# Gated linear attention and a cosine-gated MLP on one core: y evicted in token order, and output tiles stored in one transfer each

## The chip, the core and the metric

The kernel runs on one NeuronCore of a Trainium2 chip. Its engines work from queues of their own and meet at semaphores: TensorE (PE, matmuls, with PEld for the loading of weights), VectorE (DVE), ScalarE (ACT), GpSimd (POOL) and SyncE (SP), which here only issues DMA transfers. ACT and POOL can issue transfers too. The metric is the device time of a run in microseconds (us); lower is better. Differences of a few tenths of a per cent matter here.

## The reference

There are 4 batches, 8 heads, 768 tokens and a head dimension of 48. The first half is a recurrence over tokens with a state of 48 x 48 for each head; the second is an MLP over 3072 tokens of 384 features, with 2048 hidden features and a gate h * cos(h).

```
for t in range(S):
    state = alpha[:, :, t, :, None] * state + einsum('bhd,bhe->bhde', k[:, :, t], v[:, :, t])
    y[:, :, t] = einsum('bhd,bhde->bhe', q[:, :, t], state)
x = y.transpose(0, 2, 1, 3).reshape(B * S, H * D)     # tokens x 384
h = x @ w_in
out = (h * cos(h)) @ w_out                            # tokens x 384, float32
```

## The kernel before

The tokens are worked on in 12 pairs J (NJ = 12) of 256 tokens (T2), each of two chunks c of 128 tokens (C); three pairs make a batch. An input transfer (`load`, L105) puts two neighbouring tokens, an even one and an odd one (index e), into one partition. Within a chunk the tokens therefore stand in the order "64 even ones, then 64 odd ones" in everything that follows: masks, scores, y, the hidden features, and the rows of the output tile.

For each pair the attention steps are: logarithms and cumulated sums of alpha, scaling of q and k (`scale_k` L212, `scale_q` L216, on POOL or DVE), a cast of v (`cast_v`, L219, POOL) and a rearrangement of it by four SBUF transfers (`stack_v`, L225, issued by SP), transposes (`trans`, L260) and their evictions (L266), scores (L274) with a mask (L279), the state's update (`outer` L291, `add_state` L305, `decay_state` L313), and `yT` (L340), which leaves y transposed in PSUM: three groups of 128 features on the partitions, tokens along the row. `evict_y` (L350) copies one chunk of it to the bf16 tile xT, once on ACT or DVE for each chunk.

The MLP for a pair: `mlp1` (L359) multiplies w_in with xT in four parts u, ACT takes the sine with a shift of pi/2 (`cosine`, L365), DVE multiplies (`gate`, L370), and `mlp2` (L387) multiplies with w_out, chunk by chunk in four parts, with the gated tile gsb as the stationary operand, so that tokens come out on the partitions. `evict_o` (L396) copies a chunk's 128 x 384 result to SBUF, and `store` (L403) sends it to memory. As partitions 0 to 63 hold even tokens and 64 to 127 odd ones, it issues two transfers for each chunk, of 64 rows that lie two rows apart in memory.

The last chunk of all, (11, 1), is different. `mlp2` (L381) computes its left and right 192 columns apart, in the two banks of one PSUM tile o_last. In each of its four parts there are four matmuls for the left half, then four for the right. `evict_o` (L394) copies the left half on ACT and the right on DVE, into one SBUF tile, and `store` issues four transfers: the even tokens of each half on SP's queue and the odd ones on ACT's.

PSUM has a tag "h" with three tiles of two banks (`two_banks`, used for y, U, the scores, h and o_last), a tag "x" of one bank (the cumulated sums of a pair) and a tag "o" of one bank (the outputs). Each o_sb tile is one of four buffers.

The order of the work is written out by hand: a table PLAN gives every step of every pair a number, the steps are issued sorted by it, and each engine executes its own in that order. SP's queue thus holds loads, rearrangements of v and stores in one sequence: a store that waits for its eviction, or whose issue takes long, holds back the loads behind it.

Of the kernel before, what the change touches and what calls it, by code (L numbers as in the profile page):

```python
# [9 lines left out]
FP = mybir.dt.float32  # L10
# [6 lines left out]
def kernel(  # L17
# [10 lines left out]
    nc = tc.nc  # L28
    B, H, S, D = q.shape
    DM, DF = moe_w_in.shape  # L30
    C = 128
    HC = C // 2
    T2 = 2 * C
    NJB = S // T2
    NJ = B * NJB
    NP = H // 2
    HD = H * D
    KT = DM // C
# [9 lines left out]
    sb = ctx.enter_context(tc.tile_pool(name="sb", bufs=2))  # L48
    ps = ctx.enter_context(tc.tile_pool(name="ps", bufs=1, space=bass.MemoryType.PSUM))
# [14 lines left out]
    for c in range(2):  # L64
        r = slice(HC * c, HC * c + HC)
# [14 lines left out]
    for lst, nm, n in ((lna_t, "lna", NL), (kh_t, "kh", NQ), (qh_t, "qh", NQ), (vp_t, "vp", NV)):  # L80
        for r in range(n):
            t = consts.tile([C, 2, H, 64], BF, tag=f"{nm}{r}", name=f"{nm}{r}")
            nc.vector.memset(t[:, :, :, D:64], 0.0)
            lst.append(t)
    for r in range(NS):
        t = consts.tile([C, 2, H, 64], BF, tag=f"vs{r}", name=f"vs{r}")
# [8 lines left out]
    w2 = consts.tile([C, NF, DM], BF, tag="w2", name="w2")  # L95

    a_sb, kqv, cp_sb, icp_sb, qkT_sb, A_sb, c2_sb = {}, {}, {}, {}, {}, {}, {}
    xT, gsb = {}, {}
# [72 lines left out]
    def two_banks(name):  # L171
        return ps.tile([C, 2, 512], FP, tag="h", name=name, bufs=3)
# [78 lines left out]
    T_ps, A_ps, y_ps, U_ps = {}, {}, {}, {}  # L251
# [95 lines left out]
    def evict_y(J, c, copy):  # L347
        if J not in xT:
            xT[J] = sb.tile([C, KT, T2], BF, tag="xT", name="xT", bufs=BUF["xT"])
        copy(out=xT[J][:, :, c * C : (c + 1) * C], in_=y_ps[J][:, c, 0 : KT * C].rearrange("r (i t) -> r i t", i=KT))  # L350

    h_ps, c_sb, o_ps, o_sb = {}, {}, {}, {}

# [19 lines left out]
    HALVES = [slice(0, DM // 2), slice(DM // 2, DM)]  # L373

    def mlp2(J, c, part):
        if (J, c) == (NJ - 1, 1):
            if part == 0:
                o_ps[J, c] = two_banks("o_last")
            for z, cols in enumerate(HALVES):
                for ft in range(part * NF // MP, (part + 1) * NF // MP):  # L380
                    nc.tensor.matmul(o_ps[J, c][:, z, 0 : DM // 2], gsb[J][:, ft, c * C : (c + 1) * C], w2[:, ft, cols],  # L381
                                     start=(ft == 0), stop=(ft == NF - 1))
            return
        if part == 0:
            o_ps[J, c] = ps.tile([C, 512], FP, tag="o", name="o_ps", bufs=1)
        for ft in range(part * NF // MP, (part + 1) * NF // MP):
            nc.tensor.matmul(o_ps[J, c][:, 0:DM], gsb[J][:, ft, c * C : (c + 1) * C], w2[:, ft],  # L387
                             start=(ft == 0), stop=(ft == NF - 1))

    def evict_o(J, c, copy):  # L390
        o_sb[J, c] = sb.tile([C, DM], FP, tag="o_sb", name="o_sb", bufs=4)
        if (J, c) == (NJ - 1, 1):
            for z, cp in enumerate((nc.scalar.copy, nc.vector.tensor_copy)):
                cp(out=o_sb[J, c][:, HALVES[z]], in_=o_ps[J, c][:, z, 0 : DM // 2])  # L394
        else:
            copy(out=o_sb[J, c], in_=o_ps.pop((J, c))[:, 0:DM])  # L396

    def store(J, c):
        rows = out[J * T2 + c * C : J * T2 + (c + 1) * C, :].rearrange("(i e) d -> e i d", e=2)
        for cols in HALVES if (J, c) == (NJ - 1, 1) else [slice(0, DM)]:  # L400
            for e in range(2):
                eng = nc.scalar if (J, c, e) == (NJ - 1, 1, 1) else nc.sync
                eng.dma_start(out=rows[e][:, cols], in_=o_sb[J, c][HC * e : HC * e + HC, cols])  # L403

    idle_ps = []

    def idle(n):
# [12 lines left out]
        "vev": lambda J, eng="DVE": evict_vs(J, copies[eng]), "decay": decay, "trans": trans,  # L420
        "evT": lambda J, c, eng="DVE": evict_T(J, c, copies[eng]), "scores": scores, "mask": mask, "outer": outer,
        "add": add_state, "state": decay_state, "yT": yT, "evy": lambda J, c, eng="ACT": evict_y(J, c, copies[eng]),
        "m1": mlp1, "sin": cosine, "gate": gate, "m2": mlp2, "evo": lambda J, c, eng="ACT": evict_o(J, c, copies[eng]),
        "out": store, "idle": idle,
    }

# [70 lines left out]
    for key, line in PLAN.items():  # L497
        kind, *rest = key.split()
        for J, word in enumerate(line.split()):
            if word != "-":  # L500
                t, _, eng = word.partition(":")
# [38 lines left out]
```

## Time and profile before

| | us |
|---|---|
| median of 3 runs | 189.28 (189.15 to 189.62) |
| the profiled execution | 189.54 |
| its span, from first to last instruction | 187.5 |
| PE busy in the span | 176.4 |
| DVE, ACT, POOL busy | 134.8, 125.3, 77.8 |

The span is what the page and the trace show; about 2 us of the execution lie outside it. A row of "groups of instructions" gives line, engine, operation, output and inputs, shapes and count, then the busy time in us and the mean of one in ns, then the idle time of the engine just before and what ended it. In the order of time the columns are start, duration, engine, line, operation and count. For a stretch, each engine's busy time comes with the count in brackets, then the granted clock of PE, the busy share of the DMA engines (it can pass 1) and GB/s. SPq and ACTq are the queues in which SP and ACT issue transfers; the time of such a row is that of the issue, not of the transfer, whose time from issue to landing is given apart.

### The profile page before, as it was taken

What the parts mean: (1) busy time and instruction counts of PE and PEld (TensorE: products, weight loads), DVE (VectorE), ACT (ScalarE), POOL (GpSimd) and SP (SyncE); (2) the same over time, 40 slices, a digit from 0 to 9 for tenths busy, and PEclk for the clock granted to TensorE, in tenths of its full rate; (3) what the DMA queues carried; (4) which work ended last, traced back from release to release, by engine and by line L of the source; (5) the groups of instructions that cost most, each with busy time, mean ns of one, the idle gap of its engine ahead of it and who ended that gap; (6) DMA issues with size and microseconds to landing.
All of it is one profiled execution on the core that took longest, in us unless ns stands there. A gap on an engine that the chain in (4) does not pass through costs nothing.

```text
span 187.5 us, 5788 instructions
## 1 busy us (share of the span) xinstructions
PE 176.4 (94%) x2469; PEld 126.2 (67%) x2469; DVE 134.8 (72%) x184; ACT 125.3 (67%) x161; POOL 77.8 (42%) x110
## 2 busy tenths in 40 slices
PE   7888799998999999999999999999999999999990
PEld 2434678664577776775598668586776787776880
DVE  7178785589799899588748986885876766573550
ACT  2456876799598977779668999728956182372510
POOL 5079510267564733693895168830540310100000
PEclk9999999999999999999999999999999999999997
DMA  6999999999979958997699944600052004411303
GB/s 146 261 259 166 181 204 237 256 270 258 244 197 290 258 137 206 266 255 185 156 275 257 264 108 101 168 0 3 3 118 69 0 23 108 113 31 45 84 0 84
DMA packets 60537, 29.47 MB, mean 157 GB/s; under 512 B 51424, under 2 KB 60512, under 8 KB 60512
## 3 DMA queue, kind: packets, MB, share of 16 engines
q1 hardware_dynamic: 56640, 25.86, 59.8%
q0 software_dynamic: 3712, 3.15, 11.0%
q8 instruction: 19, 0.31, 0.7%
q10 hardware_dynamic: 160, 0.10, 0.2%
q14 instruction: 6, 0.05, 0.1%
HBM read 25.17 MB, written 4.72 MB: 159 GB/s over the span
## 4 chain that ended last, share of the span: by engine, by line
PE 57%; ACT 16%; DVE 7%; DMA 6%; POOL 5%; SPq 4%; issue 3%; POOLq 0%; DVEq 0%
PE h_ps L359 25%; PE o_ps L387 20%; ACT c_sb L365 4%; PE y_ps L340 3%; DMA a<-in_alpha_dram 3%; DMA v<-in_v_dram 3%; ACT qkT L266 3%; DVE gsb L370 3%; ACT L136 2%; SPq L225 2%; PE T_ps L260 2%; ACT L365 2%; PE A_ps L274 2%; ACT icp L192 2%; ACT cp L200 2%
## 5 line engine op out<-in xcount | busy, mean ns | idle before, releaser
L370 DVE TENSOR_TENSOR gsb<-h_ps,c_sb 128x1024 bf16<-128x1024 f32 x48 | 58.1, 1221 | 21.8 <-ACT c_sb L365 21.0
L365 ACT ACTIVATE c_sb<-h_ps,halfpi 128x1024 bf16<-128x1024 f32 x48 | 53.1, 1114 | 26.8 <-PE h_ps L359 22.9
L359 PE MATMUL h_ps<-xT,w 128*128 128x256 bf16 x576 | 66.7, 273 | 0.9 <-ACT xT L350 0.5
L387 PE MATMUL o_ps<-w,gsb 128*128 128x384 bf16 x368 | 66.7, 327 | 0.0
L359 PEld LDWEIGHTS <-w 128*128 128x128 bf16 x576 | 55.6, 98 | 9.9 <-issue 1.4
L387 PEld LDWEIGHTS <-gsb 128*128 128x128 bf16 x368 | 33.8, 98 | 21.2 <-DVE gsb L370 0.6
L313 POOL TENSOR_TENSOR un<-us,c 128x384 bf16<-128x384 f32 x20 | 16.7, 837 | 40.1 <-DVE us L305 33.8
L279 DVE TENSOR_TENSOR A_sb<-A_ps,msk 128x1024 bf16<-128x1024 f32 x24 | 28.9, 1217 | 1.7 <-PE A_ps L274 1.7
L212 POOL TENSOR_TENSOR kh<-k,icp 128x384 bf16<-128x384 f32 x17 | 16.9, 1000 | 8.8 <-ACT icp L192 8.8
L216 POOL TENSOR_TENSOR qh<-q,cp 128x384 bf16<-128x384 f32 x15 | 15.4, 1031 | 10.5 <-ACT cp L200 10.5
L149 POOL TENSOR_TENSOR a<-a 128x384 f32<-128x384 f32 x9 | 9.3, 1038 | 12.8 <-DMA a<-in_alpha_dram 12.8
L219 POOL CAST vp<-v 128x768 bf16<-128x768 f32 x12 | 10.1, 842 | 10.0 <-DMA v<-in_v_dram 9.9
L141 ACT ACTIVATE lna<-a 128x768 bf16<-128x768 f32 x12 | 10.2, 847 | 4.7 <-DMA a<-in_alpha_dram 4.7
L266 ACT COPY qkT<-T_ps 128x1024 bf16<-128x1024 bf16 x8 | 8.0, 1016 | 7.1 <-PE T_ps L260 4.9
L411 PE MATMUL idle_ps<-zeros 128*128 128x512 bf16 x40 | 11.5, 431 | 1.2 <-DVE zeros L52 1.2
L136 ACT ACT_TABLE_LOAD x9 | 11.5, 1283 | 0.9 <-PEq L524 0.7
L266 DVE COPY qkT<-T_ps 128x1024 bf16<-128x1024 bf16 x16 | 10.8, 683 | 1.7 <-ACT qkT L266 1.7
L365 ACT ACT_TABLE_LOAD x9 | 11.5, 1283 | 0.2
L305 DVE TENSOR_TENSOR us<-U_ps,un 128x384 f32<-128x384 f32 x16 | 8.7, 550 | 3.8 <-PE U_ps L291 2.8
L396 DVE COPY o_sb<-o_ps 128x384 f32<-128x384 f32 x12 | 6.6, 552 | 6.6 <-PE o_ps L387 6.6
L274 PE MATMUL A_ps<-qkT 48*128 48x128 bf16 x192 | 9.2, 218 | 1.0 <-ACT vs L239 0.6
L396 ACT COPY o_sb<-o_ps 128x384 f32<-128x384 f32 x11 | 5.3, 479 | 7.0 <-PE o_ps L387 5.2
(69 smaller groups left out, 155.5 us busy)
## 6 DMA issues: line engine op xcount, KB each, us to landing
k<-in_k_dram SPq DMA_DIRECT2D x12, 384.0 KB, 5.4
a<-in_alpha_dram SPq DMA_DIRECT2D x12, 384.0 KB, 5.9
v<-in_v_dram SPq DMA_DIRECT2D x12, 384.0 KB, 5.8
q<-in_q_dram SPq DMA_DIRECT2D x12, 384.0 KB, 5.9
out_dram<-o_sb SPq DMA_DIRECT2D x46, 96.0 KB, 3.1
vs<-vp SPq DMA_DIRECT2D x36, 64.0 KB, 2.3
w<-in_moe_w_out_dram POOLq DMA_DIRECT2D x4, 384.0 KB, 10.0
w<-in_moe_w_in_dram POOLq DMA_DIRECT2D x4, 384.0 KB, 7.2
```

The source lines that it names most:

```text
L136: nc.scalar.preload_act_table_set("natural_log_exp_and_others")
L212: eng.tensor_tensor(out=kh_t[J % NQ][:, e, :, 0:D], in0=kqv["k", J][:, :, e], in1=icp_, op=ALU.mult)
L216: eng.tensor_tensor(out=qh_t[J % NQ][:, e, :, 0:D], in0=kqv["q", J][:, :, e], in1=cp, op=ALU.mult)
L266: copy(out=qkT_sb[J][:, c], in_=T_ps[J][:, c].rearrange("r n e s -> r n (e s)"))
L274: nc.tensor.matmul(A_ps[J, c][:, a, p, :], qkT[r, c, NP + p, :], qkT[r, c, p, :], start=True, stop=True)
L279: nc.vector.tensor_tensor(out=A_sb[J][:, c].rearrange("s a p t -> s (a p) t"), in0=A_ps.pop((J, c)).rearrange("s a p t -> s (a p) t"), in1 ...
L313: nc.gpsimd.tensor_tensor(out=u, in0=U_sum.pop(n), in1=c2_sb[J][:, :, c].unsqueeze(3).to_broadcast([C, NP, 2, D]), op=ALU.mult)
L359: nc.tensor.matmul(h_ps[J, u][:, f, :], w1[:, kk, ft * C : (ft + 1) * C], xT[J][:, kk, :], start=(kk == 0), stop=(kk == KT - 1))
L365: nc.scalar.activation(out=c_sb[J, u], in_=h_ps[J, u], func=AF.Sin, bias=halfpi, scale=1.0)
L370: nc.vector.tensor_tensor(out=gsb[J][:, u * FW : (u + 1) * FW], in0=h_ps.pop((J, u)), in1=c_sb.pop((J, u)), op=ALU.mult)
L387: nc.tensor.matmul(o_ps[J, c][:, 0:DM], gsb[J][:, ft, c * C : (c + 1) * C], w2[:, ft], start=(ft == 0), stop=(ft == NF - 1))
L396: copy(out=o_sb[J, c], in_=o_ps.pop((J, c))[:, 0:DM])
```

## The change

`evict_y` now reads a chunk of y in its old order (64 even tokens, 64 odd ones) and writes it to xT in the order of the tokens: of 128 adjacent bf16 columns the even positions are written first, then the odd ones, so that neighbouring writes of a run are 4 bytes apart. All that follows (h, the gate, the outputs) has its tokens in order, and `store` sends a chunk as one transfer of 128 rows that lie one after another in memory.

For the last chunk, the left half's PSUM tile is now the bank of the tag "x", and the right half's is the first bank of a two-bank tile. Each half is evicted into an SBUF tile of its own (o_half), and stored by one transfer of 128 rows x 192 columns: the left one issued by ACT, the right one by SP. The order of steps is as before.

```diff
     def evict_y(J, c, copy):
         ...
-        copy(out=xT[J][:, :, c * C : (c + 1) * C], in_=y_ps[J][:, c, 0 : KT * C].rearrange("r (i t) -> r i t", i=KT))
+        copy(out=xT[J][:, :, c * C : (c + 1) * C].rearrange("r i (t e) -> r i e t", e=2),
+             in_=y_ps[J][:, c, 0 : KT * C].rearrange("r (i e t) -> r i e t", i=KT, e=2))
 
     def mlp2(J, c, part):
         if (J, c) == (NJ - 1, 1):
             if part == 0:
-                o_ps[J, c] = two_banks("o_last")
+                o_ps[J, c] = [ps.tile([C, 512], FP, tag="x", name="o_last", bufs=1), two_banks("o_last")[:, 0]]
             for z, cols in enumerate(HALVES):
                 for ft in range(part * NF // MP, (part + 1) * NF // MP):
-                    nc.tensor.matmul(o_ps[J, c][:, z, 0 : DM // 2], gsb[J][:, ft, c * C : (c + 1) * C], w2[:, ft, cols],
+                    nc.tensor.matmul(o_ps[J, c][z][:, 0 : DM // 2], gsb[J][:, ft, c * C : (c + 1) * C], w2[:, ft, cols],
                                      start=(ft == 0), stop=(ft == NF - 1))
 
     def evict_o(J, c, copy):
-        o_sb[J, c] = sb.tile([C, DM], FP, tag="o_sb", name="o_sb", bufs=4)
         if (J, c) == (NJ - 1, 1):
+            o_sb[J, c] = []
             for z, cp in enumerate((nc.scalar.copy, nc.vector.tensor_copy)):
-                cp(out=o_sb[J, c][:, HALVES[z]], in_=o_ps[J, c][:, z, 0 : DM // 2])
+                t = sb.tile([C, DM // 2], FP, tag=f"o_half{z}", name="o_half", bufs=1)
+                cp(out=t, in_=o_ps[J, c][z][:, 0 : DM // 2])
+                o_sb[J, c].append((t, HALVES[z], (nc.scalar, nc.sync)[z]))
         else:
-            copy(out=o_sb[J, c], in_=o_ps.pop((J, c))[:, 0:DM])
+            t = sb.tile([C, DM], FP, tag="o_sb", name="o_sb", bufs=4)
+            copy(out=t, in_=o_ps.pop((J, c))[:, 0:DM])
+            o_sb[J, c] = [(t, slice(0, DM), nc.sync)]
 
     def store(J, c):
-        rows = out[J * T2 + c * C : J * T2 + (c + 1) * C, :].rearrange("(i e) d -> e i d", e=2)
-        for cols in HALVES if (J, c) == (NJ - 1, 1) else [slice(0, DM)]:
-            for e in range(2):
-                eng = nc.scalar if (J, c, e) == (NJ - 1, 1, 1) else nc.sync
-                eng.dma_start(out=rows[e][:, cols], in_=o_sb[J, c][HC * e : HC * e + HC, cols])
+        rows = out[J * T2 + c * C : J * T2 + (c + 1) * C, :]
+        for t, cols, eng in o_sb.pop((J, c)):
+            eng.dma_start(out=rows[:, cols], in_=t)
```

## The prediction

> **What bounds the kernel now.** I read first the table of busy times and the slices, then the busy times in stretches of 4 us, then the chain of waits at the end, then the queues.
>
> ```profile
> PE 176.4 (94%) x2469; PEld 126.2 (67%) x2469; DVE 134.8 (72%) x184; ACT 125.3 (67%) x161; POOL 77.8 (42%) x110
> PE   7888799998999999999999999999999999999990
> PEclk9999999999999999999999999999999999999997
> ```
>
> TensorE (PE) works 176.4 of 187.5 us, at full granted clock up to the last slice. Its instruction order is fixed, so only a gap in that row can be won back. The stretches that hold gaps after the first output store (45 us), and one in which another resource is thin:
>
> ```profile
> core 0: us, PE busy (x) PEld busy (x) DVE busy (x) ACT busy (x) POOL busy (x), PEclk, DMA share, GB/s
> 44.00:48.00 4.00, 3.54 (x37) 2.04 (x36) 4.00 (x6) 3.40 (x7) 2.48 (x4) 1.00 1.12 255
> 48.00:52.00 4.00, 3.55 (x126) 2.49 (x124) 3.00 (x5) 2.41 (x5) 2.71 (x4) 1.00 0.92 238
> 68.00:72.00 4.00, 4.00 (x64) 2.72 (x64) 3.69 (x4) 1.88 (x4) 0.00 (x0) 1.00 0.40 90
> 80.00:84.00 4.00, 3.73 (x59) 2.83 (x57) 3.60 (x5) 3.06 (x4) 4.00 (x5) 1.00 1.14 253
> 84.00:88.00 4.00, 3.65 (x49) 2.28 (x48) 3.05 (x4) 3.97 (x7) 0.91 (x3) 1.00 0.79 210
> 116.00:120.00 4.00, 3.69 (x38) 2.69 (x37) 2.51 (x4) 3.51 (x4) 4.00 (x7) 1.00 0.48 106
> 180.00:184.00 4.00, 3.25 (x28) 2.31 (x26) 1.25 (x3) 0.32 (x1) 0.00 (x0) 1.00 0.07 17
> ```
>
> The reader sees two kinds of place: gaps of 0.3 to 0.5 us in the middle, and the end, where PE stops at 183.26 and the last 4.2 us are eviction, stores and the closing steps. The end, by the chain, the order of time, the source line of the stores (two stretches of it, with the time from issue to landing) and the page's table of DMA issues (count, size, median us to landing):
>
> ```profile
> 181.93 1.33 PE o_last L381 x16
> ...
> 183.29 0.33 ACT o_sb L394
> ...
> 183.64 0.36 DVE o_sb L394
> ...
> 182.55 2.56 SPq L403 DMA_DIRECT2D out_dram<-o_sb  x4
> 183.64 1.21 ACTq L403 DMA_DIRECT2D out_dram<-o_sb  x2
> ...
> L403 SPq DMA_DIRECT2D out_dram<-o_sb x2: 466/531/596, 182.6 to 183.1; - x2
> ...
> DMA to landing us min/median/max: 2.1/2.1/2.2
> ...
> L403 SPq DMA_DIRECT2D out_dram<-o_sb x1: 710/710/710, 184.4 to 184.4; - x1
> ...
> DMA to landing us min/median/max: 2.1/2.1/2.1
> ...
> out_dram<-o_sb SPq DMA_DIRECT2D x46, 96.0 KB, 3.1
> out_dram<-o_sb ACTq DMA_DIRECT2D x2, 48.0 KB, 2.0
> ```
>
> ACT evicts the left half only when all 16 matmuls are done, DVE the right half only when ACT is done, and SP, still issuing the piece before, issues the last piece at 184.4. It lands 2.1 us later, at 186.5; 1.0 us of closing steps follows to 187.5.
>
> **The change, part by part: the end.** (a) The halves get PSUM tiles of their own. The last 16 matmuls take 1.33 us, 0.083 us each; the left half's last is the fifth from the end, so ACT may start 4 x 0.083 = 0.33 us earlier, at 182.96. That is not on the path: the right half is later. (b) The halves get SBUF tiles of their own, so DVE no longer waits for ACT and starts where ACT did, right behind PE: 183.29 in place of 183.64, a gain of 0.35. It ends at 183.65. (c) Before, between the end of DVE's eviction (183.64 + 0.36 = 184.00) and the last issue (184.4) lie 0.4 us in which SP still issues the piece ahead. Now SP has one issue for the tile before (from 182.55, at most 0.71 us, so free by 183.26) and issues the right half at once, at 183.67; the left half goes through ACT's queue at about 183.31. Together the last issue moves from 184.4 to 183.67: a gain of 0.73. (d) That piece now has 128 partitions and 96 KB where it had 64 and 48 KB. The 96 KB pieces at 182.6 landed in 2.1 to 2.2 us, against 2.1 for the 48 KB piece: a cost of 0 to 0.1, and I allow another 0.1 for the left half's transfer beside it. Sum at the end: a gain of 0.53 to 0.73; I take 0.65, since the 2.1 us of a piece hardly moves with its size.
>
> The Trainium skill (SBUF — State Buffer, Door 1: The DMA port swizzle) says that a transfer from 64 partitions of one half reaches 8 of 16 SBUF ports and one from 128 reaches all. By that rule the doubled piece would cost nothing more and the sum at the end would be 0.73; the rows above, with 0 to 0.1 for the doubled bytes, do not exclude it.
>
> **The queue of SP.** 24 of 48 SP issues and one of two ACT issues go, and with each the issue time.
>
> ```profile
> L403 SPq DMA_DIRECT2D out_dram<-o_sb x48: 466/595/1790, 45.2 to 184.4; - x48
> ...
> 65.52 4.00 SPq L225 DMA_DIRECT2D vs<-vp  x4
> 69.56 1.24 SPq L403 DMA_DIRECT2D out_dram<-o_sb  x2
> 70.84 0.59 SPq L105 DMA_DIRECT2D a<-in_alpha_dram  x1
> 71.48 0.69 SPq L105 DMA_DIRECT2D v<-in_v_dram  x1
> ...
> 76.82 0.83 POOL L219 CAST vp<-v 128x768 bf16<-128x768 f32 x1 [2.55 <-DMA v<-in_v_dram]
> 82.40 0.99 POOL L216 TENSOR_TENSOR qh<-q,cp 128x384 bf16<-128x384 f32 x1
> ...
> 83.45 0.41 PE L260 MATMUL T_ps<-ident_bf,qh 64*128 64x64 bf16 x16 [0.27 <-POOL qh L216]
> ```
>
> 24 x 0.595 = 14 us of SP time go, but SP is not the bound; what counts is where a load behind a store is waited for. One place shows: at 66 to 72 us the DMA engines are at 0.40 because SP issues back to back; the load of v behind it lands at 76.7, POOL waits 2.55 us for it, then works without a pause to 83.39, and PE waits 0.27 us for POOL's qh. One store issue less puts the v load 0.6 us earlier, POOL 0.6 earlier (its 2.55 us of waiting covers that), and the gap of 0.27 closes. The gain is 0 (if the a load issued just ahead takes the bandwidth, or another input holds POOL or PE) to 0.27; past that, DVE and ACT hand on the next piece and nothing is won. I take 0.25, because the chain has no slack in it. The other gaps have no store ahead of them on their way: 44 to 52 us has DVE at 4.00 of 4.00 and then evictions. The most that could come in the middle is the sum of the gaps after 68 us, 0.27 + 0.35 + 0.31 = 0.93. Bytes do not change (192 KB a tile), so the transfers themselves are costed at nothing.
>
> **The evictions of y.** As many instructions on the same engines; only the step of the writes changes, from 2 to 4 bytes, in 3 x 2 runs of 64. The reads in PSUM stay contiguous, and the matmuls read xT as before.
>
> ```profile
> L350 DVE CAST xT<-y_ps 128x384 bf16<-128x384 f32 x12 | 6.5, 553 | 4.5 <-PE y_ps L340 2.9 <-ACT xT L350 1.5
> L396 DVE COPY o_sb<-o_ps 128x384 f32<-128x384 f32 x12 | 6.6, 552 | 6.6 <-PE o_ps L387 6.6
> L279 DVE TENSOR_TENSOR A_sb<-A_ps,msk 128x1024 bf16<-128x1024 f32 x24 | 28.9, 1217 | 1.7 <-PE A_ps L274 1.7
> L350 ACT CAST xT<-y_ps 128x384 bf16<-128x384 f32 x12 | 5.5, 481 | 5.5 <-PE y_ps L340 3.8 <-DVE xT L350 1.6
> L266 ACT COPY qkT<-T_ps 128x1024 bf16<-128x1024 bf16 x8 | 8.0, 1016 | 7.1 <-PE T_ps L260 4.9 <-DVE qkT L266 2.2
> ...
> 22.11 4.16 PE L359 MATMUL h_ps<-xT,w 128*128 128x256 bf16 x36 [0.51 <-ACT xT L350]
> 51.63 0.51 PE L291 MATMUL U_ps<-vp,kh 64*128 64x96 bf16 x16 [0.45 <-DVE xT L350]
> 75.92 0.56 DVE L350 CAST xT<-y_ps 128x384 bf16<-128x384 f32 x1 [0.54 <-ACT xT L350]
> 76.53 1.47 PE L359 MATMUL h_ps<-xT,w 128*128 128x256 bf16 x12
> ```
>
> On DVE a write of 2-byte elements (553 ns) costs what one of 4-byte elements does (552 ns): it runs at (1217 - 553) / 640 = 1.04 ns per element and gains nothing from neighbours that could now be lost. ACT runs at (1016 - 481) / 640 = 0.84 ns. No row shows 2-byte writes with a step. From below the change is 0 (no reason for a faster write); from above I bound it at a doubled cost per element, + 384 x 1.04 = 0.40 us (DVE) and + 384 x 0.84 = 0.32 us (ACT), 0.72 for a pair in sequence. I take 0, from the equal DVE rows.
>
> The Trainium skill (SBUF — State Buffer, Door 1, the remark on cachelines) says that steps are free while at least two accesses fall into one 16-byte line; four would here, so by it too the sum stands. No run here shows such a write yet.
>
> **Sum.** 0.65 + 0.25 = 0.90 less. The profiled execution took 189.54, 0.26 over the median of 189.28, with 2.0 us outside the span; its span would be 186.6 and its time 188.64, which on the median is 188.4.
>
> **Rivals.** (1) The end gains, the middle does not: the v load comes earlier but PE waits for something else, as the gap at 86.8 (0.35 in 84 to 88) would remain anyway. 189.28 - 0.65 = 188.6. (2) The middle gains more, as loads spread earlier past every store: up to 0.93 in place of 0.25, 187.7; against it, the rows quoted show a load behind only the first of them. (3) No measurable change (the change does not do what it says): the two 96 KB halves, side by side behind a third piece of 192 KB, land up to 0.4 us later, as two pieces in the profile's crowded stretches do (the median store landing is 3.1 us against 2.1 at the end), and the middle gives nothing: 189.28 - 0.73 + 0.4 = 188.95. (4) Slower: the stepped write of y is dear. PE waits directly on xT at 22.11 and 51.63, and the pair that ends at 75.92 + 0.56 = 76.48 has PE's next matmuls on xT 0.05 us behind it; three exposed pairs at 0.72 give 2.16, so 189.28 - 0.90 + 2.16 = 190.5. The three pairs are 3 x 768 = 2304 elements; it decides from 0.90 / 2304 = 0.39 ns more per element. Against it, the equal DVE rows. (5) Slower by order: the earlier loads take bandwidth from one that PE needs sooner (stretches with a DMA share over 1.0 are common), and one more gap like the 0.45 at 51.63 opens twice: 189.28 - 0.65 + 0.9 = 189.5, against it that no issue on SP comes later than before.
>
> The Trainium skill (DMA: Bandwidth & Descriptors, Issuing engines are not separate DMA queues) says that transfers issued by SP and ACT share the same engines and that two queues save issue time only. That would bear out the third rival's crowding, though in the profile the pieces from ACT and SP at the end, side by side, landed in 2.0 and 2.1 us.
>
> **Chances.** Forecast 0.38, (1) 0.20, (2) 0.07, (3) 0.19, (4) 0.09, (5) 0.07. A change of under 0.3% (0.57 us, so 188.71 to 189.85) is about what a measurement of this kernel can tell from none. Faster is the forecast, (2) and nearly all of (1): 0.63. Same is (3), the rest of (1) and most of (5): 0.26. Slower is (4) and the rest of (5): 0.11. The range goes from 187.8 (near the whole of rival 2) to 189.3 (rival 3 and its scatter); left out are (4), most of (5) and the edge of (2), under 0.2.
>
> **What would show it.** After: DVE's right half starts within 0.05 us behind PE's last matmul and waits for PE, not ACT; SP's last issue follows DVE at once; the last landing comes about 2.2 us later and 1.0 us ahead of the end. 24 SP store issues of 192 KB and about 0.6 us each, landing 2 to 5 us later. The xT rows stay at 481 and 553 ns; over 600 shows rival 4. The wait of T_ps for POOL's qh near 83 us is gone, and busy PE ends about 0.25 earlier (183.0); if PE ends at 183.26 or later, the middle step failed. The prediction is wrong if the last pieces land in over 2.5 us, or a new gap shows in PE between 45 and 120 us.

## The result, and the profile after

The changed kernel takes 188.25 us (median of 6 runs, 187.93 to 188.33) against 189.22 us for the kernel before beside it: a ratio of 0.9946, 95% interval 0.9932 to 0.9960. In two later comparisons it stood at 0.9962 (0.9946 to 0.9977) and 0.9975 (0.9958 to 0.9993). The gain is real and small, 0.5 to 1.0 us. The time was forecast; the way there was so only in part, and that the number hit owes much to luck.

The profiled execution has a span of 186.5 us, 1.0 less than before. The end of the changed kernel, by the order of time, and the source line of its stores in the last stretch:

```profile
181.91 1.48 PE L384 MATMUL o_last<-w,gsb 128*128 128x192 bf16 x16
...
182.70 0.33 SPq L408 DMA_DIRECT2D out_dram<-o_sb  x1
183.10 0.32 ACT L398 COPY o_half<-o_last 128x192 f32<-128x192 f32 x1 [3.88 <-PE o_last L384]
183.43 0.36 DVE L398 COPY o_half<-o_last 128x192 f32<-128x192 f32 x1 [0.76 <-PE o_last L384]
183.45 0.37 ACTq L408 DMA_DIRECT2D out_dram<-o_half  x1
183.82 0.33 SPq L408 DMA_DIRECT2D out_dram<-o_half  x1
...
L408 SPq DMA_DIRECT2D out_dram<-o_half x1: 332/332/332, 183.8 to 183.8; - x1
...
DMA to landing us min/median/max: 1.6/1.7/1.7
```

ACT starts 0.33 us ahead of DVE, each waits for PE alone, and SP issues the right half 0.03 us after DVE ends. The issue takes 0.33 us where the last one took 0.71, and the piece lands 1.6 us after its issue where it took 2.1. PE's work, however, ends 0.14 us later than before (DVE behind it starts at 183.43, where ACT started at 183.29). So the whole gain and more lies behind PE's last matmul: from there to the end of the span it is 186.5 - 183.43 = 3.07 us, and was 187.5 - 183.29 = 4.21. This "last stretch" (from the start of the first eviction that needs all of PE's work to the end of the span) is what the experiments below are compared by, since it hardly varies (3.07 to 3.16 us in three profiles of the changed kernel; spans are given to 0.1 us), while the end of PE's work varies by several tenths from one profile to the next.

The groups of instructions that evict y, and PE's waits that have to do with them (order of time, the wait in brackets):

```profile
L351 DVE CAST xT<-y_ps 128x384 bf16<-128x384 f32 x12 | 6.8, 584 | 4.7 <-PE y_ps L340 2.9 <-ACT xT L351 1.8
L351 ACT CAST xT<-y_ps 128x384 bf16<-128x384 f32 x12 | 6.7, 594 | 5.6 <-PE y_ps L340 3.8 <-DVE xT L351 1.8
...
22.20 4.09 PE L361 MATMUL h_ps<-xT,w 128*128 128x256 bf16 x36 [0.65 <-ACT xT L351]
41.66 0.41 PE L260 MATMUL T_ps<-ident_bf,qh 64*128 64x64 bf16 x16 [0.61 <-DVE qh L216]
52.07 0.51 PE L291 MATMUL U_ps<-vp,kh 64*128 64x96 bf16 x16 [0.59 <-DVE xT L351]
77.09 1.47 PE L361 MATMUL h_ps<-xT,w 128*128 128x256 bf16 x12 [0.26 <-DVE xT L351]
83.58 0.40 PE L260 MATMUL T_ps<-ident_bf,qh 64*128 64x64 bf16 x16
```

The eviction takes 594 ns on ACT (481 before) and 584 on DVE (553). PE's waits for xT grow at 22 and 52 us by 0.14 each, and a new one of 0.26 stands at 77. The wait for POOL's qh at 83 us, 0.27 before, is gone.

### The profile page after: what moved, and what is told of

The parts are those of the page before. It is cut to its first block, busy times and chain, and to the rows that moved or that the text cites. A ratio compares the mean times of both kernels' runs of the same rounds, so it can differ in the third digit from the quotient of the medians.

```text
span 186.5 us, 5746 instructions
## 1 busy us (share of the span) xinstructions
PE 176.7 (95%) x2467; PEld 126.4 (68%) x2469; DVE 135.4 (73%) x184; ACT 126.5 (68%) x161; POOL 77.1 (41%) x110
## 4 chain that ended last, share of the span: by engine, by line
PE 73%; ACT 15%; DVE 8%; issue 3%; DVEq 0%
PE h_ps L361 31%; PE o_ps L390 24%; PE idle_ps L416 4%; PE y_ps L340 3%; ACT qkT L266 3%; DVE gsb L372 3%; PE T_ps L260 2%; ACT c_sb L367 2%; PE A_ps L274 2%; ACT L136 2%; ACT cp L200 2%; PE U_ps L291 2%; DVE kh L212 2%; ACT icp L192 2%; PE o_last L384 1%
## 5 line engine op out<-in xcount | busy, mean ns | idle before, releaser
L416 PE MATMUL idle_ps<-zeros 128*128 128x512 bf16 x38 | 12.0, 457 | 1.4 <-DVE zeros L52 1.2
L351 ACT CAST xT<-y_ps 128x384 bf16<-128x384 f32 x12 | 6.7, 594 | 5.6 <-PE y_ps L340 3.8
L351 DVE CAST xT<-y_ps 128x384 bf16<-128x384 f32 x12 | 6.8, 584 | 4.7 <-PE y_ps L340 2.9
```

Source lines behind the costliest of these rows:

```text
L351: copy(out=xT[J][:, :, c * C : (c + 1) * C].rearrange("r i (t e) -> r i e t", e=2), in_=y_ps[J][:, c, 0 : KT * C].rearrange("r (i e t) -> ...
L416: nc.tensor.matmul(idle_ps[0], zeros[:, 0:C], zeros, start=True, stop=True)
```

## The experiments

**Own tiles alone.** The kernel before, with the last chunk's halves in PSUM and SBUF tiles of their own and the four stores as they were.

```diff
-                o_ps[J, c] = two_banks("o_last")
+                o_ps[J, c] = [ps.tile([C, 512], FP, tag="x", name="o_last", bufs=1), two_banks("o_last")[:, 0]]
...
-                cp(out=o_sb[J, c][:, HALVES[z]], in_=o_ps[J, c][:, z, 0 : DM // 2])
+                t = sb.tile([C, DM // 2], FP, tag=f"o_half{z}", name="o_half", bufs=1)
+                cp(out=t, in_=o_ps[J, c][z][:, 0 : DM // 2])
```

> The kernel before, with only the last tile's halves in PSUM and SBUF tiles of their own; y stays in its old order and each piece of 64 rows has its own store. Theory (the end was bound by SP's queue of issues as much as by DVE's wait for ACT): DVE evicts the right half 0.35 us earlier, but SP still issues two pieces of the tile before (from 182.55), then the left piece, then the right one, which cannot start before 184.3 in place of 184.4; the time stays within 0.1 us of 189.2. Rival (DVE's wait for ACT was the bound, as the prediction booked 0.35 us for it): 188.85.

Measured: 189.2 us, ratio 0.9984 (0.9965 to 1.0004). The kernel before stood at 189.4 us beside it, so the time alone cannot tell the theory (a ratio near 1) from the rival (188.85 / 189.22 = 0.998); the trace can. The end of it, by the order of time:

```profile
182.50 1.11 SPq L408 DMA_DIRECT2D out_dram<-o_sb  x2
182.90 0.32 ACT L395 COPY o_half<-o_last 128x192 f32<-128x192 f32 x1 [3.88 <-PE o_last L381]
183.23 0.36 DVE L395 COPY o_half<-o_last 128x192 f32<-128x192 f32 x1 [0.76 <-PE o_last L381]
183.25 1.28 ACTq L408 DMA_DIRECT2D out_dram<-o_half  x2
183.70 1.19 SPq L408 DMA_DIRECT2D out_dram<-o_half  x2
```

DVE no longer waits for ACT, but SP is at the left half from 183.70 and comes to the right one only behind it. The last stretch is 187.3 - 183.23 = 4.07 us, 0.14 less than before. Alone, the tiles bring little: SP's queue stood ready to take the place of the wait removed.

**Token order alone.** The changed kernel with one PSUM tile and one SBUF tile for the last chunk.

```diff
-                o_ps[J, c] = [ps.tile([C, 512], FP, tag="x", name="o_last", bufs=1), two_banks("o_last")[:, 0]]
+                o_ps[J, c] = two_banks("o_last")
...
-                t = sb.tile([C, DM // 2], FP, tag=f"o_half{z}", name="o_half", bufs=1)
-                cp(out=t, in_=o_ps[J, c][z][:, 0 : DM // 2])
-                o_sb[J, c].append((t, HALVES[z], (nc.scalar, nc.sync)[z]))
+                cp(out=t[:, HALVES[z]], in_=o_ps[J, c][:, z, 0 : DM // 2])
+                o_sb[J, c].append((t[:, HALVES[z]], HALVES[z], (nc.scalar, nc.sync)[z]))
```

> The changed kernel with the last tile's halves back in one PSUM tile and one SBUF tile; token order and one store for each tile or half stay. Theory: ACT waits for all 16 matmuls again and DVE for ACT, so the last issue comes 0.35 us later than in the changed kernel (184.17 where it has 183.82) and the time is 188.25 + 0.35 = 188.6. Together with the tiles-only run this would show that the two parts of the end add up only jointly. Rival (the halves' transfers side by side cost as much): 188.25.

Measured: 188.91 us, ratio 0.9963 (0.9942 to 0.9984), which holds both the theory's 188.6 / 189.22 = 0.9967 and the rival's 0.9949. The evictions, by the order of time:

```profile
183.04 0.32 ACT L398 COPY o_sb<-o_last 128x192 f32<-128x192 f32 x1 [4.21 <-PE o_last L384]
...
183.39 0.36 DVE L398 COPY o_sb<-o_last 128x192 f32<-128x192 f32 x1 [1.11 <-ACT o_sb L398]
```

The last stretch is 186.5 - 183.04 = 3.46 us: 0.75 less than before without the tiles, and the tiles then bring another 0.39 (to 3.07). So with the stores whole the tiles are worth 0.39 us (0.35 by the rows: DVE starts 0.35 us behind ACT here and at PE's last matmul in the changed kernel), and with the stores in pieces 0.14.

**The step taken out.** The changed kernel with the old, contiguous eviction.

```diff
-        copy(out=xT[J][:, :, c * C : (c + 1) * C].rearrange("r i (t e) -> r i e t", e=2),
-             in_=y_ps[J][:, c, 0 : KT * C].rearrange("r (i e t) -> r i e t", i=KT, e=2))
+        copy(out=xT[J][:, :, c * C : (c + 1) * C], in_=y_ps[J][:, c, 0 : KT * C].rearrange("r (i t) -> r i t", i=KT))
```

> The changed kernel with the old contiguous eviction of y, so that the rows of the output come out in the order of even tokens, then odd ones; all else as changed. Theory (the step of 4 bytes costs 0.11 us on ACT and 0.03 us on DVE, PE pays for it at 22, 52 and 77 us, and this ate the 0.25 us won at 83 us): xT rows back at 481 and 553 ns, PE's last matmul ends at 183.0 where the changed kernel has 183.41, time 187.85. Rival (the middle moved for reasons of the queue, not of the evictions): PE ends at 183.4, time 188.25.

**The step alone.** The same edit the other way round, in the kernel before.

> The kernel before with only the stepped eviction of y; the stores stay as before, so that the rows of the output come out in another order. Theory: xT rows of 594 and 584 ns; PE falls back by 0.4 to 0.6 us up to 77 us, but it then waits less for POOL's qh at 83 us, which hangs on the load of v and not on PE, so that 0.1 to 0.2 us remain: 189.22 + 0.15 = 189.4. Rival (the cost adds up at each exposed pair and is carried to the end): 189.8. If the xT rows stay at 481 and 553 ns, the longer evictions come from something else in the change.

Measured: without the step 188.36 us, ratio 0.9931 (0.9904 to 0.9958); with the step alone 189.74 us, ratio 1.0018 (0.9995 to 1.0042). The xT rows follow the edit: 553 and 480 ns without the step, 584 and 594 with it, whatever the stores. The last stretch does not: 3.08 us without the step (the changed kernel: 3.07), 4.19 with the step alone (before: 4.21). The expected end of PE at 183.0 did not show in the first: its profile has waits of its own, one of 0.49 us for a load of weights at 25 us and one of 0.79 us at 100 us. Its ratio agrees with the theory (187.85 / 189.22 = 0.9928), but the interval holds the rival's 0.9949 too. The time of the second, at plus 0.18%, leaves theory and rival undecided; its trace bears out the theory for the middle. PE's work at 77, 83 and 86 us with the step alone, and then the last of these in the kernel before:

```profile
76.94 1.47 PE L360 MATMUL h_ps<-xT,w 128*128 128x256 bf16 x12 [0.26 <-DVE xT L350]
...
83.43 0.40 PE L260 MATMUL T_ps<-ident_bf,qh 64*128 64x64 bf16 x16
...
86.79 0.52 PE L291 MATMUL U_ps<-vp,kh 64*128 64x96 bf16 x16 [0.35 <-DVE gsb L371]
...
86.82 0.52 PE L291 MATMUL U_ps<-vp,kh 64*128 64x96 bf16 x16 [0.35 <-DVE gsb L370]
```

PE is 0.41 us late at 77 us (76.53 before), and level again at 86. The wait for POOL's qh at 83 us is gone although every store is still in two pieces: PE comes later, and here POOL is also earlier, as the v load is issued at 70.69 us in place of 71.48. So that wait's absence in the changed kernel does not by itself show that the shorter queue helped.

**Whole stores cut in two again.** The changed kernel with each store as two of 64 partitions, now of adjacent rows.

```diff
-            eng.dma_start(out=rows[:, cols], in_=t)
+            for e in range(2):
+                eng.dma_start(out=rows[HC * e : HC * e + HC, cols], in_=t[HC * e : HC * e + HC, :])
```

> The changed kernel with each store cut into two of 64 partitions again, now of adjacent rows in memory. Theory (a store of 64 partitions takes longer to issue than one of 128, whatever the rows): issue 0.55 to 0.6 us and 2.0 to 2.1 us to land at the end as in the kernel before, the stretch after PE's last matmul 0.9 us longer than in the changed kernel, time 189.1. Rival (the pitch of two rows in memory made the issue slow): issue 0.33 us and 1.6 us to land, the stretch at most 0.4 us longer, time 188.6.

**The changed kernel beside it.**

> The changed kernel again, beside the next three on one chip. 0.9946 of the kernel before; the stretch from PE's last matmul to the end of the span is 3.1 us, whenever PE ends.

Measured: in two pieces 189.37 us, ratio 1.0011 (0.9997 to 1.0026); the changed kernel beside it 188.45 us, 0.9962 (0.9946 to 0.9977). Of the first, the groups at the source line of the stores from 184.6 us on (issue in ns, least, median and most, then the time to landing), and two rows in the order of time:

```profile
L409 SPq DMA_DIRECT2D out_dram<-o_half x2: 548/573/598, 184.1 to 184.7; - x2
...
DMA to landing us min/median/max: 2.0/2.0/2.1
...
183.63 0.36 DVE L398 COPY o_half<-o_last 128x192 f32<-128x192 f32 x1 [0.76 <-PE o_last L384]
...
184.10 1.19 SPq L409 DMA_DIRECT2D out_dram<-o_half  x2
```

Pieces of 64 adjacent rows are issued and landed as slowly as those two rows apart were: the pitch is not the cause. The last stretch is 187.7 - 183.63 = 4.07 us, as with the tiles alone. The whole stores are worth 1.0 us there: the last issue starts 1.07 us behind the start of DVE's eviction in place of 0.39 (ahead of it are the issue of the other piece, 0.55 to 0.6 us, and 0.1 in which SP is not yet done with the tile before), and its piece lands 2.0 us after it in place of 1.6. With the stores in two pieces, own tiles and token order together are no faster than the kernel before. The changed kernel's own second profile has 186.1 - 183.01 = 3.09 us, with PE done 0.42 us earlier than in its first.

**The reordering moved.** Two ways to have token order without a stepped write: the read in PSUM jumps, or PE's moving operand in `yT` does and the eviction is contiguous on both sides, as in the kernel before (the second diff leaves that line out).

```diff
-        copy(out=xT[J][:, :, c * C : (c + 1) * C].rearrange("r i (t e) -> r i e t", e=2),
-             in_=y_ps[J][:, c, 0 : KT * C].rearrange("r (i e t) -> r i e t", i=KT, e=2))
+        copy(out=xT[J][:, :, c * C : (c + 1) * C].rearrange("r i (t e) -> r i t e", e=2),
+             in_=y_ps[J][:, c, 0 : KT * C].rearrange("r (i e t) -> r i t e", i=KT, e=2))
```

> The changed kernel with the reordering on the reading side of the eviction of y: the writes to xT are contiguous, the reads in PSUM jump between the 64 even and the 64 odd tokens of a chunk. If the extra 0.11 us (ACT) and 0.03 us (DVE) come from the step of the writes, and reads in PSUM may jump freely, the xT rows are back at 481 and 553 ns and the kernel gains what the step costs, about 0.3 us on the changed one (ratio 0.993). If jumping reads are dearer than stepped writes, the rows pass 600 ns and it is slower than the changed kernel.

```diff
-                        todo.append((c, g, i, U[:, p, 32 * x : 32 * x + 32], qkT[:, c, p, :]))
+                        todo.append((c, g, i, U[:, p, 32 * x : 32 * x + 32], qkT[:, c, p, :].rearrange("r (e t) -> r t e", e=2)))
...
-                            todo.append((c, g, i, vf[:, 128 * p + d : 128 * p + d + 32], A[:, c, a, p, :]))
+                            todo.append((c, g, i, vf[:, 128 * p + d : 128 * p + d + 32], A[:, c, a, p, :].rearrange("s (e t) -> s t e", e=2)))
```

> The changed kernel with the reordering in yT: its matmuls read their moving operand (qkT, A_sb) with jumps, so that y comes out in token order and its eviction is contiguous on both sides. If PE reads jumping columns at no cost, the xT rows are at 481 and 553 ns, y's matmuls stay at 0.9 us for 56 and the ratio is 0.993. If each jumping read costs PE, y's matmuls get longer; at a doubled pace 12 x 0.9 us more, about 10 us slower.

Measured: the jumping read 187.87 us, ratio 0.9931 (0.9911 to 0.9952); the jumping moving operand 196.7 us, ratio 1.0394 (1.0372 to 1.0416). The groups of the first that evict y, and its PE, POOL and PE again in the order of time:

```profile
L351 DVE CAST xT<-y_ps 128x384 bf16<-128x384 f32 x12 | 6.5, 553 | 4.5 <-PE y_ps L340 2.9 <-ACT xT L351 1.5
L351 ACT CAST xT<-y_ps 128x384 bf16<-128x384 f32 x12 | 5.5, 481 | 5.5 <-PE y_ps L340 3.8 <-DVE xT L351 1.6
...
51.59 0.52 PE L291 MATMUL U_ps<-vp,kh 64*128 64x96 bf16 x16 [0.45 <-DVE xT L351]
...
75.27 0.83 POOL L219 CAST vp<-v 128x768 bf16<-128x768 f32 x1 [1.04 <-PE y_ps L340]
...
86.35 0.52 PE L291 MATMUL U_ps<-vp,kh 64*128 64x96 bf16 x16 [0.35 <-DVE gsb L372]
98.99 4.75 PE L361 MATMUL h_ps<-xT,w 128*128 128x256 bf16 x42 [0.32 <-issue]
```

The evictions are back at their old times, the wait at 77 us is gone, and the one at 52 is as before. The same matmul group at 86 us starts at 86.35 here, and in the changed kernel's profile taken beside it at:

```profile
86.78 0.52 PE L291 MATMUL U_ps<-vp,kh 64*128 64x96 bf16 x16 [0.35 <-DVE gsb L372]
```

Beside whole stores, the step thus cost PE 0.43 us by then. It is not there at the end of these two profiles: PE stands still for 0.32 us at 99 us with the jumping read and not with the stepped write, and at 120 us they are level, at 119.67 and 119.65 us; both spans are 186.1 us. Jumping reads cost PE's moving operand dearly instead: the two groups of y's matmuls, 7.4 and 5.6 us in the changed kernel (its first group stands first here), become 14.0 and 9.6:

```profile
L340 PE MATMUL y_ps<-A_sb,vs 128*32 128x128 bf16 x384 | 7.4, 219 | 0.0
...
L340 PE MATMUL y_ps<-A_sb,vs 128*32 128x128 bf16 x384 | 14.0, 285 | 0.0
L340 PE MATMUL y_ps<-qkT,un 128*32 128x128 bf16 x240 | 9.6, 286 | 0.2 <-ACT qkT L266 0.2
```

**The pair again.** The jumping read and the changed kernel, once more side by side.

> The changed kernel once more, to set the jumping read beside it on another chip: 0.995 to 0.996 of the kernel before.

> The jumping read again. Theory (it saves what the stepped write costs PE at 22, 52 and 77 us): 0.3 us under the changed kernel, 0.993 of the kernel before. Rival (the difference of the first pair was scatter): the same ratio as the changed kernel.

Measured: 187.98 us, ratio 0.9955 (0.9938 to 0.9972), for the jumping read; 188.51 us, 0.9975 (0.9958 to 0.9993), for the changed kernel. The intervals touch each time, but the medians lie 0.58 and 0.53 us apart, in the same order: by the medians the jumping read is the best of the three versions. That it saves PE the waits for xT is in the traces; that these make up the whole difference is not shown.

**The price of the step by itself.**

```diff
         for _, _, kind, args in sorted(order, key=lambda x: x[:2]):
             steps[kind](*args)
+        ...
+        for _ in range(3):
+            for cp in (nc.scalar.copy, nc.vector.tensor_copy):
+                cp(out=wide[:, 0:384], in_=flat)                                                   # L522
+                cp(out=wide[:, 0:768].rearrange("p (n s) -> p s n", s=2)[:, 0], in_=flat)          # L523
+                cp(out=wide[:, 0:1536].rearrange("p (n s) -> p s n", s=4)[:, 0], in_=flat)         # L524
+                cp(out=wide[:, 0:384].rearrange("p (i t e) -> p i e t", i=3, e=2), ...)            # L525
+                cp(out=wide[:, 0:480].rearrange("p (i t) -> p i t", i=6)[:, :, 0:64], ...)         # L526
+                cp(out=wide_f[:, 0:384], in_=flat)                                                 # L527
+                cp(out=wide_f[:, 0:768].rearrange("p (n s) -> p s n", s=2)[:, 0], in_=flat)        # L528
+                cp(out=wide[:, 0:384].rearrange("p (i t e) -> p i t e", i=3, e=2), ...)            # L529
```

> The changed kernel with 48 copies of 384 elements from PSUM behind its last step, three of each of eight forms on ACT and on DVE: contiguous bf16 writes; a step of 4 bytes; a step of 8 bytes; the change's form (3 x 2 runs of 64 with a step of 4 bytes); six contiguous runs of 64 with gaps between; contiguous float32; float32 with a step of 8 bytes; contiguous bf16 writes with the reads jumping. Only the rows of these copies are read; the time is longer by them. If the cost is one per element of the step, the change's form and the plain step of 4 bytes take the same, 0.11 us (ACT) and 0.03 us (DVE) over the contiguous one, and runs with gaps cost nothing. If it is one per run, the six contiguous runs cost the same as the change's form and the plain step nothing.

The groups of these copies, three of each (line, then busy us and mean ns of one behind the bar; the line numbers in the diff are added here):

```profile
L524 ACT CAST wide<-src_ps 128x384 bf16<-128x384 f32 x3 | 3.0, 1008 | 0.1
L524 DVE CAST wide<-src_ps 128x384 bf16<-128x384 f32 x3 | 3.0, 1007 | 0.1
...
L523 ACT CAST wide<-src_ps 128x384 bf16<-128x384 f32 x3 | 1.8, 586 | 0.1
L525 ACT CAST wide<-src_ps 128x384 bf16<-128x384 f32 x3 | 1.8, 585 | 0.1
L525 DVE CAST wide<-src_ps 128x384 bf16<-128x384 f32 x3 | 1.8, 585 | 0.1
L523 DVE CAST wide<-src_ps 128x384 bf16<-128x384 f32 x3 | 1.8, 583 | 0.1
...
L528 DVE COPY wide_f<-src_ps 128x384 f32<-128x384 f32 x3 | 1.7, 558 | 0.1
L522 DVE CAST wide<-src_ps 128x384 bf16<-128x384 f32 x3 | 1.7, 558 | 13.9 <-ACT wide L529 13.9
L526 DVE CAST wide<-src_ps 128x384 bf16<-128x384 f32 x3 | 1.7, 557 | 0.1
L529 DVE CAST wide<-src_ps 128x384 bf16<-128x384 f32 x3 | 1.6, 547 | 0.0
L527 DVE COPY wide_f<-src_ps 128x384 f32<-128x384 f32 x3 | 1.6, 547 | 0.0
...
L528 ACT COPY wide_f<-src_ps 128x384 f32<-128x384 f32 x3 | 1.5, 497 | 0.1
L527 ACT COPY wide_f<-src_ps 128x384 f32<-128x384 f32 x3 | 1.5, 485 | 0.0
L529 ACT CAST wide<-src_ps 128x384 bf16<-128x384 f32 x3 | 1.4, 480 | 0.0
L522 ACT CAST wide<-src_ps 128x384 bf16<-128x384 f32 x3 | 1.4, 479 | 10.5 <-DVE wide L529 10.0 <-PE src_ps L516 0.4
L526 ACT CAST wide<-src_ps 128x384 bf16<-128x384 f32 x3 | 1.4, 479 | 0.1
```

Against the contiguous copy (L522) the plain step of 4 bytes (L523) costs what the change's form does (L525), and six contiguous runs (L526) cost nothing: the price hangs on the step. Jumping reads (L529) are free on both engines.

## Why the prediction was right, and where it was wrong

**The end (booked 0.65 us, measured 1.14 by the last stretch).** Steps (a), (b) and (c) came as written: ACT starts 0.33 us ahead, DVE right behind PE, and SP's last issue follows the start of DVE's eviction by 0.39 us (predicted 183.67 - 183.29 = 0.38). The mis-sized term is (d). It took the landing time of 96 KB from rows of 64 partitions, 2.1 to 2.2 us, and added 0.1 for the neighbour; a store of 128 partitions lands 1.6 us after its issue, 0.5 us less where up to 0.2 more was booked. That is nearly all the difference: 0.73 + 0.5 = 1.23, against 1.14. The sentence from the Trainium skill (SBUF — State Buffer, Door 1: The DMA port swizzle) pointed the right way, with nothing to pay for the doubled bytes. That the issue gets shorter by 0.22 to 0.38 us, which is part of that 0.5 as the landing is counted from the start of the issue, was not foreseen.

The working gave (b) a gain of its own, 0.35. The runs with one part each show that it hangs on (c): 0.14 us for the tiles by themselves, 0.75 for the order and whole stores, 1.14 together.

**The queue of SP (booked 0.25).** In the profiles the mechanism works without the step and is worth nothing with it. The v load that POOL waits for is issued at 70.61 us in place of 71.48 and lands 5.0 us later; POOL starts on it at 75.76 in place of 76.82. (Where a row names PE's y_ps as what POOL waited for, as the jumping read's does, the start still follows the load's landing: 70.32 + 4.8 = 75.1 us there, and 75.27. The issue also moves by itself: 70.69 to 71.95 us in the four profiles with stores in two pieces, 69.95 to 70.91 in the eight with whole ones.) With the jumping read PE's matmul group at 86 us starts at 86.35 where it started at 86.82: 0.47 us, the wait of 0.27 and most of the rest because the two transposing groups there overlap when there is no wait (0.24 us from start to start, for 0.41 us of each). With the stepped write that group starts at 86.79 and 86.88 with stores in two pieces and at 86.78 to 87.00 in five profiles with whole ones. The step makes PE late, PE finds qh ready in either case, and the earlier load is not waited for any more. The 0.25 rested on PE coming to qh as early as before.

**The evictions of y (booked 0).** This is the step that failed. "I take 0, from the equal DVE rows" compared contiguous 2-byte with contiguous 4-byte writes, which says nothing about a step. A pair costs 0.113 + 0.031 = 0.144 us, a fifth of the upper bound of 0.72, and PE pays for it at the three places that rival 4 named: 0.14 at 22 us, 0.14 at 52 and 0.12 to 0.15 at 77 (0.26 us of idle time where 0.11 stood before, with no wait named), together the 0.41 us by which PE is late at 77 with the step alone. Rival 4's mechanism was at work, at 0.144 us / 768 elements = 0.19 ns per element, under the 0.39 from which it would have decided.

**The sum.** Booked were 0.65 + 0.25 + 0 = 0.90. The profiled pair shows 1.14 at the end and -0.14 ahead of it, 1.00 together. The forecast of 188.4 hit 188.25 by luck: the end was too small by 0.49, and the middle too favourable by 0.39. Of the stories that the prediction told, rival 1 (the end gains, the middle does not) is nearest to what happened, with rival 4's step as the reason. Two signs that the prediction set came out against it: PE ends after 183.26 (183.41), and a new gap shows between 45 and 120 us (0.26 at 77). The xT rows neither stayed at 481 and 553 ns nor passed 600.

**What stays open.** The new wait of 0.61 us for DVE's qh at 41.7 us shows in 4 of 7 profiles with the stepped write and in none of 5 with contiguous writes and the old moving operand. What it is can be read from DVE and POOL, first in the changed kernel's first profile, which has the wait, then in its second, which has not:

```profile
39.78 1.82 DVE L216 TENSOR_TENSOR qh<-q,cp 128x384 bf16<-128x384 f32 x2
40.16 1.02 POOL L149 TENSOR_TENSOR a<-a 128x384 f32<-128x384 f32 x1 [0.72 <-DMA a<-in_alpha_dram]
...
39.82 1.01 DVE L216 TENSOR_TENSOR qh<-q,cp 128x384 bf16<-128x384 f32 x2
40.34 1.36 POOL L149 TENSOR_TENSOR a<-a 128x384 f32<-128x384 f32 x1 [0.86 <-DMA a<-in_alpha_dram]
```

In the four profiles with the wait POOL starts 0.35 to 0.40 us behind the first of DVE's two products, and these take 1.82 us; in the other eight it starts 0.49 to 1.07 us behind, and they take 1.01 or 1.02, while POOL's instruction takes up to 1.39. The step brings DVE there about 0.1 us later, but POOL's start, which hangs on the load of alpha, varies by more; so the step may make the wait likelier, which is not shown. Little of it is left later: PE's group at 86 us starts at 86.88 to 87.00 with it and at 86.78 to 86.82 without (in profiles with the stepped write).

At 99 us PE stands still for 0 to 1.06 us with nothing named ("issue"), in kernels of both kinds, and in all three profiles with whole stores, contiguous writes and the old moving operand (0.32, 0.34 and 0.79); why is open. So what the middle is worth at the end of the span cannot be read from single profiles: the 0.47 and 0.43 stand at 86 us. The medians say that the changed kernel gains 0.55 to 0.97 us, less than the 1.14 of its end, and that the jumping read gains 0.53 to 0.58 more; this is somewhat over the 0.43, and the profiles do not show where the rest comes from.

## What to carry to other kernels

Follow a removed wait to the next queue on the same path: DVE's wait for ACT was worth 0.14 us while SP had two stores to issue per tile and 0.39 us once it had one. A wait that is gone is not yet a gain: PE's wait for qh at 83 us went when POOL came earlier, and also where PE came later, and the two do not add. Before an access pattern is booked at nothing, find a row with the same step and width on the same side, or put both ends into the range; and try the jump on the side where it is free, here the PSUM reads of ACT and DVE and neither the SBUF writes nor PE's moving operand. Compare small changes by a stretch that does not vary from run to run, not by where a long schedule happens to end.

## What the runs showed of the hardware that was not expected

At the quiet end of the kernel a store of 128 partitions is issued in 0.33 to 0.37 us and lands 1.6 to 1.9 us after the start of its issue; one of 64 partitions with half the bytes takes 0.47 to 0.71 us and 2.0 to 2.3, adjacent rows or not. Over the whole run the medians of the issue are 0.53 and 0.595 us. From PSUM to SBUF, a 2-byte write with a step of 4 bytes runs at 585 ns for 384 elements on ACT and on DVE alike, and with 8 bytes at 1008 ns, where contiguous ones take 480 and 553 to 558. A 4-byte write with a step of 8 bytes costs 0.01 us over the contiguous one. The Trainium skill (SBUF — State Buffer, Door 1, the remark on cachelines) has both steps of the 2-byte writes free, with four and two accesses to a line; the runs do not agree (585 and 1008 ns), and the measurement decides. Copies that read PSUM in jumps of 64 elements pay nothing, while matmuls whose moving operand jumps so take 285 in place of 219 ns each, and 23.6 in place of 13.0 us of busy time for 624 of them. Two products on DVE take 1.82 in place of 1.01 us when an instruction on POOL starts 0.35 to 0.40 us behind the first of them.
